# Staged loads in four transfers, g over h in PSUM, and three banks for h: linear attention and a cosine feed-forward layer in one kernel

## The chip, the cores and the metric

The kernel runs on one core of a Trainium2 chip. The metric is the device time of one execution in microseconds (us). The engines are TensorE (PE, matrix products into PSUM), VectorE (DVE), ScalarE (ACT), GpSimd (POOL) and SyncE (SP, which here issues most of the DMA transfers). PSUM has eight banks of 512 fp32 words per partition.

## The reference

The first half is a recurrent linear attention over 768 tokens, with 4 batches of 8 heads of 48 dimensions. The second half is a feed-forward layer on its output, laid out as 3072 tokens by 384.

```
for t in range(S):
    kt, vt, rt = k[:, :, t], v[:, :, t], r[:, :, t]
    cur = einsum('bhd,bhe->bhde', u * kt, vt)
    y[:, :, t] = einsum('bhd,bhde->bhe', rt, state + cur)
    state = w * state + einsum('bhd,bhe->bhde', kt, vt)
x = y as (B*S, H*D)
h = x @ w_in            # 3072 x 384 by 384 x 2048
g = h * cos(h)
out = g @ w_out         # 2048 x 384
```

The weights w_in and w_out come as 64-bit floats; everything else is fp32.

## The kernel before, in words

**Feed-forward.** Each fp32 factor is split into a high and a low part in the type fp32r, and three products replace one. The 24 chunks of 128 tokens form eight blocks of three. A step is one block and one slice f of 128 of the 2048 hidden columns, so there are 128 steps. The first four blocks are walked in four groups of slices (CUTS, L31), so that weights can be converted while the work goes on; the other four take all 16 slices at once. A step is:

- `h` (mm_h, L322): nine matmuls into one PSUM bank, the buffer `ph`
- `qi` on ACT (L342) and `rest` on DVE (L345): h/2pi less its whole part, into `q`, a slot of the SBUF ring `f`
- `cos` on ACT (L348), in place in `q`
- the gate on DVE (f_gate, L1240): g = `ph` times `q`, written over `q` (a block of two chunks would write over `ph`; there is none)
- `gh` on ACT (L1243): g rounded to fp32r; `gl` on DVE (L1246): g less `gh`
- `o` (mm_o, L333): nine matmuls that add the step's share to three accumulator banks

After a block's last slice of a group the accumulators are copied to slots of the ring `f` (L1280 on ACT, L1282 on DVE) and stored by SP, or added to the output by POOL (L1296).

**Attention.** Chunks 0 to 11 (`chunk`, L702) hold 128 tokens of one batch. Chunks 12 to 23 (`late_chunk`, L918) hold 64 tokens of each of two batches. A late chunk needs k and r transposed, with head dimensions on partitions. It loads them in a second, *staged* form (load_s, L940) into slots of the ring `raw`, which has two slots and also serves the weights. DVE transposes them in 32x32 blocks (tr_s, L977, the transpose itself at L980), and POOL multiplies the decay in (decay_s, L984 and L987). The plain loads of k, r and v (load, L931, issued at L934) follow in SP's queue; r goes to a slot of the ring `f`. POOL makes the bonus from them (L999, L1002) and decays k (L1005). PE makes the scores and the state's increment (mm_az, L1035), DVE masks the scores (L1072), and PE makes x (mm_xx, L1095), which ACT and DVE split (L1141, L1146).

**Staged layout.** For each of four 32-row groups n and each batch b, one transfer fills 16 partitions, each with 4 tokens of four heads: 64 pieces of 768 bytes, eight transfers per tensor. In the last chunk the last transfer would run past the tensor's end, so POOL clears a corner (L960) and that transfer is cut into three.

**PSUM.** Banks 0 to 2 are accumulators. h uses banks 3, 4 and 5 in blocks 0 to 3 (B_HX) and banks 3 and 4 in blocks 4 to 7 (B_H). Late attention uses a pair of banks, 5-6 or 6-7 (P_ATT); single banks for small work come from 5 to 7 (B_ATT). The early chunks take any of seven banks (B_EARLY).

**Order.** Every piece of work is an `op` (L90) with an engine, a due time, a cost, a latency, and the buffers it uses. The class `Plan` simulates the engines at build time and hands out buffers by the simulated time at which they are free. `order` (L179) makes 60 tries: after the first ones, `change` (L201) shifts the due times of the best so far at random, for ops due before time 120; each try is replayed with random delays (`replay`, L159), and the best is kept. Its order is written into the instruction streams, so each engine runs its instructions strictly in this order. An op with `port=True` is planned not to overlap another such op, on DVE or POOL. The staged loads are planned with cost 3.9 and latency 3.0, the plain ones with 1.3 and 2.6.

```
P_ATT = [Tile(bank_all[:, i : i + 2], bank[i : i + 2]) for i in (5, 6)]
B_ACC, B_H, B_ATT = bank[0:3], bank[3:5], bank[5:8]
B_HX = bank[3:6]
```

Of the kernel before, what the change touches and what calls it, by code (L numbers as in the profile page):

```python
# [262 lines left out]
def kernel(  # L263
# [17 lines left out]
    P = 128  # L281
# [36 lines left out]
    def f32(ap):  # L318
        return ap.bitcast(F32)
# [31 lines left out]
    with ExitStack() as actx:  # L351
# [4 lines left out]
        bank = [Tile(bank_all[:, i]) for i in range(8)]  # L356
        P_ATT = [Tile(bank_all[:, i : i + 2], bank[i : i + 2]) for i in (5, 6)]
        B_ACC, B_H, B_ATT = bank[0:3], bank[3:5], bank[5:8]
        B_HX = bank[3:6]
        B_EARLY = bank[5:8] + bank[3:5] + bank[0:2]  # L360
# [334 lines left out]

        def staged(buf):
            return f32(buf()).rearrange("q f w -> q (f w)").rearrange("q (p x) -> q p x", p=NP)

# [219 lines left out]
        def late_chunk(i, due, xbuf):  # L918
# [21 lines left out]
            def load_s(buf, src):  # L940
                def part(n, b, q, n_q, p, n_p, n_d):
                    j, d0 = n // 2, 32 * (n % 2)
                    at = 32 * n + 16 * b + q
                    nc.sync.dma_start(  # L944
                        staged(buf)[at : at + n_q, p : p + n_p, 0:n_d],
                        bass.AP(
                            tensor=src.tensor,
                            offset=src.offset + (((2 * m + b) * H + 2 * p + j) * S + t0 + 4 * q) * D + d0,
                            ap=[[4 * D, n_q], [2 * S * D, n_p], [1, n_d]],
                        ),  # L950
                    )

                def go():
                    for n in range(4):
                        for b in range(2):
                            if i < NJ - 1 or n < 3 or b == 0:
                                part(n, b, 0, 16, 0, NP, 4 * D)
                            else:

                                nc.gpsimd.memset(staged(buf)[96:P, NP - 1, 4 * D - 32 :], 0.0)  # L960
                                part(n, b, 0, 16, 0, NP - 1, 4 * D)
                                part(n, b, 0, 15, NP - 1, 1, 4 * D)
                                part(n, b, 15, 1, NP - 1, 1, 4 * D - 32)

                return go
# [4 lines left out]
            ahead = [last_A[0]]  # L970
            l_ks = op(SP, due - 6.2, 3.9, load_s(ks, k), ahead, [ks], lat=3.0, line="late")
            l_rs = op(SP, due - 6.1, 3.9, load_s(rs, r), ahead, [rs], lat=3.0, line="late")
            l_k = op(SP, due - 5.2, 1.3, load(kb, k), ahead, [kb], lat=2.6, line="late")
# [3 lines left out]
            def tr_s(dst, src):  # L977
                def go():
                    blocks = staged(src).rearrange("q p (g x) -> q p g x", g=4)[:, :, :, 0:32]
                    nc.vector.transpose(dst().rearrange("q p (t g) -> q p g t", g=4), blocks)  # L980

                return go

            def decay_s(dst, dec):  # L984
                def go():
                    d = dst()[0:KP].rearrange("q p (b t) -> q p b t", b=2)
                    nc.gpsimd.tensor_tensor(  # L987
                        d, d, dec[0:KP, :, None, mid].to_broadcast([KP, NP, 2, CT]), op=ALU.mult
                    )

                return go
# [43 lines left out]
            def mm_az():  # L1035
                for p in range(NP):
                    for j in range(2):
                        ps = slice(j * DP, j * DP + D)
                        for b in range(2):
                            nc.tensor.matmul(  # L1040
                                score(j)[half[b], p, :],
                                kT()[ps, p, half[b]],
                                rT()[ps, p, half[b]],
                                start=True,
                                stop=True,
                            )
# [48 lines left out]
            def mm_xx():  # L1095
                x = xp()[:, :, 0 : NK * CT].rearrange("q b (kk t) -> q b kk t", kk=NK)
                for kk in range(NK):
                    for b in range(2):
                        for g in range(4 * kk, 4 * kk + 4):
                            p, s = divmod(g, 3)  # L1100
                            gs = slice(G * (g % 4), G * (g % 4) + G)
                            nc.tensor.matmul(  # L1102
                                x[gs, b, kk, :],
                                zb()[:, b, p, G * s : G * s + G],
                                rT()[0:KP, p, half[b]],
                                start=(kk == 0),
                                stop=False,
                                skip_group_check=True,
                            )
# [91 lines left out]
        for s, (n, f, f0, f1) in enumerate(steps):  # L1201
# [21 lines left out]
            for t, cs in enumerate(cols):  # L1223
# [12 lines left out]

                g = ph if nt == 2 else q

# [13 lines left out]
                o6 = op(ACT, dd + 1.2, 0.42 * one, f_gh, [o5], [g, gh], line="gh")  # L1252
                o7 = op(DVE, dd + 1.4, 0.48 * one, f_gl, [o6], [g, gh, gl], line="gl", port=g is q, lat=0.35)
                gs_.setdefault(s, []).append(o7)
# [211 lines left out]
```

## Time and profile before

| | |
|---|---|
| median of 3 runs | 514.33 us (514.09 to 515.32) |
| profiled execution | 515.86 us |
| its span, first to last instruction | 514.1 us |
| PE, DVE, ACT, POOL busy | 500.0, 384.7, 332.3, 175.6 us |
| mean granted TensorE clock | 0.996 |
| bytes moved by DMA | 61.74 MB in 117319 packets |

Busy time counts an instruction from its start to its end, and neighbouring instructions of PE and DVE overlap, so a busy engine may still have short waits inside. In a timeline row the columns are start and duration in us, engine, line and operation, output and inputs, shape and count; a bracket gives the idle time of the engine before it and what ended it. In the table by stretches each engine's busy time stands with its number of instructions, then the granted clock, the DMA share and GB/s. A group row ends in busy us, mean ns of one, and the idle time before them with its releasers.

### The profile page before, as it was taken

Reading aid. Unit: us, or ns where it says so; the run is one execution under the profiler, and the core shown is the slowest. Engines: PE = TensorE matmul, PEld = TensorE weight load, DVE = VectorE, ACT = ScalarE, POOL = GpSimd, SP = SyncE. Lnnn points to the kernel's source line nnn. Section 1 sums busy time; section 2 is a strip of 40 time slices with the busy share of each in tenths; the row PEclk is TensorE's granted clock in tenths of the full one; section 3 lists DMA queues with packets and bytes.
Section 4 is the critical chain, followed back from the end, with each engine's and each line's share of the span. In section 5 each row is a group of like instructions: output and inputs, shape, how many; then the busy total and the mean of one; then the engine's idle time right before and its main releaser. Section 6 shows DMA issues by size and latency. Waiting matters only on the chain.

```text
span 514.1 us, 14178 instructions
## 1 busy us (share of the span) xinstructions
PE 500.0 (97%) x5464; PEld 476.3 (93%) x5464; DVE 384.7 (75%) x777; ACT 332.3 (65%) x834; POOL 175.6 (34%) x186
## 2 busy tenths in 40 slices
PE   8899999999999999999999999999999999999995
PEld 6688899999999999999989999999999899889994
DVE  6789988889988877667786877777766776577552
ACT  3899987776777756547565765666756657375452
POOL 6767522265345443224325134132241322400000
PEclk9999999999999999999999999999999999999998
DMA  8997345478664576325666665374553653520001
GB/s 139 190 186 145 71 140 185 138 157 168 137 134 113 140 143 118 55 59 80 155 114 155 133 161 135 85 193 113 143 136 94 185 121 98 149 58 24 1 1 50
DMA packets 117319, 61.74 MB, mean 120 GB/s; under 512 B 80765, under 2 KB 113150, under 8 KB 117246
## 3 DMA queue, kind: packets, MB, share of 16 engines
q1 hardware_dynamic: 111982, 53.60, 42.8%
q0 software_dynamic: 5184, 7.08, 10.0%
q8 instruction: 44, 0.72, 0.6%
q14 instruction: 29, 0.24, 0.2%
q10 hardware_dynamic: 80, 0.10, 0.1%
HBM read 48.96 MB, written 11.80 MB: 118 GB/s over the span
## 4 chain that ended last, share of the span: by engine, by line
PE 78%; DMA 6%; DVE 4%; ACT 4%; issue 2%; SPq 2%; POOL 1%; DVEq 0%; ACTq 0%; POOLq 0%
PE bank L337 34%; PE bank L331 33%; PE bank L815 2%; DMA raw<-in_r_dram 1%; PE bank L1102 1%; PE bank L1124 1%; SPq L944 1%; ACT A L805 1%; PE bank L741 1%; PE bank L849 1%; DMA f<-in_r_dram 1%; DMA v<-in_v_dram 1%; DVE f L345 1%; PE bank L1040 1%; PE bank L836 1%
## 5 line engine op out<-in xcount | busy, mean ns | idle before, releaser
L337 PE MATMUL bank<-w_out_hi,gh 128*128 128x384 f32 x384 | 132.0, 344 | 0.6 <-DVE f L1282 0.6
L331 PE MATMUL bank<-xh,w_in_hi 128*128 128x384 f32 x384 | 129.8, 338 | 1.9 <-DVE f L1240 1.9
L337 PE MATMUL bank<-w_out_hi,gl 128*128 128x384 f32 x384 | 130.0, 338 | 0.2 <-DVE gl L1246 0.2
L331 PE MATMUL bank<-xh,w_in_lo 128*128 128x384 f32 x384 | 129.5, 337 | 0.0
L337 PE MATMUL bank<-w_out_lo,gh 128*128 128x384 f32 x384 | 129.4, 337 | 0.0
L331 PE MATMUL bank<-xl,w_in_hi 128*128 128x384 f32 x384 | 128.7, 335 | 0.0
L348 ACT ACTIVATE f<-f 128x384 f32<-128x384 f32 (+1 forms) x132 | 67.4, 513 | 49.2 <-DVE f L345 48.6
L1246 DVE TENSOR_TENSOR gl<-f,gh 128x384 fp32r<-128x384 f32 (+1 forms) x132 | 81.8, 621 | 22.6 <-ACT gh L1243 22.1
L345 DVE SCALAR_TENSOR_TENSOR f<-bank,qi 128x384 f32<-128x384 f32 (+1 forms) x132 | 71.0, 540 | 34.0 <-ACT qi L342 29.3
L342 ACT ACTIVATE qi<-bank 128x384 int32<-128x384 f32 (+1 forms) x132 | 62.7, 478 | 47.4 <-PE bank L331 46.6
L1240 DVE TENSOR_TENSOR f<-bank,f 128x384 f32<-128x384 f32 (+1 forms) x132 | 70.9, 540 | 28.4 <-ACT f L348 26.5
L1243 ACT CAST gh<-f 128x384 fp32r<-128x384 f32 (+1 forms) x132 | 65.7, 500 | 40.7 <-DVE f L1240 39.8
L331 PEld LDWEIGHTS bank<-xh,w_in_hi 128*128 128x128 f32 x384 | 72.1, 188 | 3.5 <-DVE f L1240 2.9
L337 PEld LDWEIGHTS bank<-w_out_hi,gh 128*128 128x128 f32 x384 | 72.0, 187 | 3.3 <-DVE f L1282 0.9
L337 PEld LDWEIGHTS bank<-w_out_hi,gl 128*128 128x128 f32 x384 | 72.0, 188 | 0.9 <-DVE gl L1246 0.9
L331 PEld LDWEIGHTS bank<-xh,w_in_lo 128*128 128x128 f32 x384 | 72.1, 188 | 0.0
L331 PEld LDWEIGHTS bank<-xl,w_in_hi 128*128 128x128 f32 x384 | 72.1, 188 | 0.0
L337 PEld LDWEIGHTS bank<-w_out_lo,gh 128*128 128x128 f32 x384 | 72.0, 188 | 0.0
L667 POOL TENSOR_TENSOR f<-f,raw 128x384 int32<-128x384 int32 x32 | 34.8, 1087 | 62.0 <-DVE f L656 43.7
L987 POOL TENSOR_TENSOR kT<-kT,decT_k 112x512 f32<-112x512 f32 x12 | 15.6, 1298 | 103.6 <-DVE kT L980 103.5
L1296 POOL DMA_DIRECT2D out_dram<-f x36 | 33.2, 1019 | 31.8 <-ACT f L1280 23.1
L805 ACT ACTIVATE A<-ident,a 128x128 f32<-128x128 f32 x96 | 30.2, 392 | 3.4 <-DVE a L796 3.4
(112 smaller groups left out, 617.5 us busy)
## 6 DMA issues: line engine op xcount, KB each, us to landing
raw<-in_moe_w_in_dram SPq DMA_DIRECT2D x32, 384.0 KB, 3.8
raw<-in_moe_w_out_dram SPq DMA_DIRECT2D x32, 384.0 KB, 3.8
out_dram<-f POOLq DMA_DIRECT2D x36, 192.0 KB, 4.3
raw<-in_k_dram SPq DMA_DIRECT2D x95, 48.0 KB, 2.6
raw<-in_r_dram SPq DMA_DIRECT2D x95, 48.0 KB, 2.1
k<-in_k_dram SPq DMA_DIRECT2D x12, 192.0 KB, 3.7
r<-in_r_dram SPq DMA_DIRECT2D x12, 192.0 KB, 4.6
v<-in_v_dram SPq DMA_DIRECT2D x12, 192.0 KB, 5.0
```

The lines of the kernel that those rows point to most:

```text
L331: nc.tensor.matmul(ph, a, b_, start=(i == 0), stop=(i == len(mm) - 1))
L337: nc.tensor.matmul(acc, a[:, ts], b_[:, f, :], start=(first and i == 0), stop=(last and i == 2))
L342: nc.scalar.activation(qi, ph, AF.Copy, scale=INV_2PI, bias=0.25)
L345: nc.vector.scalar_tensor_tensor(q, ph, INV_2PI, qi, op0=ALU.mult, op1=ALU.subtract)
L348: nc.scalar.activation(q, q, AF.Sin, scale=TWO_PI, bias=0.5 * math.pi)
L667: lambda: nc.gpsimd.tensor_tensor(ai(), ai(), cn(), op=ALU.add),
L805: nc.scalar.activation(A[j]()[:, p, :], ident, AF.Copy, scale=ab()[:, h : h + 1])
L987: nc.gpsimd.tensor_tensor(d, d, dec[0:KP, :, None, mid].to_broadcast([KP, NP, 2, CT]), op=ALU.mult)
L1240: nc.vector.tensor_tensor(g()[:, cs], ph()[:, cs], q()[:, cs], op=ALU.mult)
L1243: nc.scalar.copy(gh()[:, cs], g()[:, cs])
L1246: nc.vector.tensor_tensor(gl()[:, cs], g()[:, cs], f32(gh())[:, cs], op=ALU.subtract)
L1296: nc.gpsimd.dma_start(to, ob()[rows], accum_op=ALU.add)
```

## The change

There are three edits, in one kernel.

- Staged loads: a partition holds two tokens of eight heads, four of each of the chunk's two batches. The transpose needs 32 words of each token, so a piece reaches from the first of these to the last, D + 32 = 80 words (320 bytes). One transfer per group n fills 32 partitions with 8 such pieces each: four transfers per tensor instead of eight, six instead of ten in the last chunk. The transposed tiles kT and rT are now ordered by batch, pair and token instead of pair, batch and token; the same bytes are read by the decay and the matmuls through other strides. The planned cost is 2.2 instead of 3.9 and the latency 3.5 instead of 3.0.
- The gate writes g over h in PSUM for every step. `gh` and `gl` read it there, so `ph` is held until `gl`, and the slot of `q` is free after the gate. `gl` is no longer planned with `port=True`.
- Banks: h has 3, 4 and 7 for all blocks; late attention has the pair 5-6; B_ATT is 5 and 6.

```diff
-        P_ATT = [Tile(bank_all[:, i : i + 2], bank[i : i + 2]) for i in (5, 6)]
-        B_ACC, B_H, B_ATT = bank[0:3], bank[3:5], bank[5:8]
-        B_HX = bank[3:6]
+        P_ATT = [Tile(bank_all[:, 5:7], bank[5:7])]
+        B_ACC, B_H, B_ATT = bank[0:3], bank[3:5] + bank[7:8], bank[5:7]
+        B_HX = B_H
...
-                def part(n, b, q, n_q, p, n_p, n_d):
-                    j, d0 = n // 2, 32 * (n % 2)
-                    at = 32 * n + 16 * b + q
+                def part(n, e, n_e, q, n_q, n_d):
                     nc.sync.dma_start(
-                        staged(buf)[at : at + n_q, p : p + n_p, 0:n_d],
+                        pieces(buf)[32 * n + q : 32 * n + q + n_q, e : e + n_e, 0:n_d],
...
-                            ap=[[4 * D, n_q], [2 * S * D, n_p], [1, n_d]],
+                            ap=[[2 * D, n_q], [2 * S * D, n_e], [1, n_d]],
...
-                        for b in range(2):
-                            if i < NJ - 1 or n < 3 or b == 0:
-                                part(n, b, 0, 16, 0, NP, 4 * D)
+                        if i < NJ - 1 or n < 3:
+                            part(n, 0, H, 0, 32, D + 32)
+                        else:
+                            nc.gpsimd.memset(pieces(buf)[96:P, H - 1, 2 * D - 32 : D + 32], 0.0)
+                            part(n, 0, H - 1, 0, 32, D + 32)
+                            part(n, H - 1, 1, 0, 31, D + 32)
+                            part(n, H - 1, 1, 31, 1, 2 * D - 32)
...
-            l_ks = op(SP, due - 6.2, 3.9, load_s(ks, k), ahead, [ks], lat=3.0, line="late")
-            l_rs = op(SP, due - 6.1, 3.9, load_s(rs, r), ahead, [rs], lat=3.0, line="late")
+            l_ks = op(SP, due - 6.2, 2.2, load_s(ks, k), ahead, [ks], lat=3.5, line="late")
+            l_rs = op(SP, due - 6.1, 2.2, load_s(rs, r), ahead, [rs], lat=3.5, line="late")
...
-                    blocks = staged(src).rearrange("q p (g x) -> q p g x", g=4)[:, :, :, 0:32]
-                    nc.vector.transpose(dst().rearrange("q p (t g) -> q p g t", g=4), blocks)
+                    blocks = pieces(src).rearrange("q e (g x) -> q e g x", g=2)[:, :, :, 0:32]
+                    to = dst().rearrange("q p c -> q (p c)").rearrange("q (e t g) -> q e g t", e=H, g=2)
+                    nc.vector.transpose(to, blocks)
...
-                g = ph if nt == 2 else q
+                g = ph
...
-                    o7 = op(DVE, dd + 1.4, 0.48 * one, f_gl, [o6], [g, gh, gl], line="gl", port=g is q, lat=0.35)
+                    o7 = op(DVE, dd + 1.4, 0.48 * one, f_gl, [o6], [g, gh, gl], line="gl", lat=0.35)
```

More of the change, by code (lines that the diff above doesn't have):

```diff
@@ L694, in heads, with pieces, late_t @@
             return buf().rearrange("q (h d) -> q h d", h=H)
-        def staged(buf):
-            return f32(buf()).rearrange("q f w -> q (f w)").rearrange("q (p x) -> q p x", p=NP)
+        def pieces(buf):
+            return f32(buf()).rearrange("q f w -> q (f w)").rearrange("q (e x) -> q e x", e=H)
+        def late_t(buf):
+            return buf().rearrange("q p c -> q (p c)").rearrange("q (b p t) -> q b p t", b=2, p=NP)
         def cube(buf):
@@ L940, in load_s @@
             def load_s(buf, src):
-                def part(n, b, q, n_q, p, n_p, n_d):
-                    j, d0 = n // 2, 32 * (n % 2)
-                    at = 32 * n + 16 * b + q
+                def part(n, e, n_e, q, n_q, n_d):
                     nc.sync.dma_start(
-                        staged(buf)[at : at + n_q, p : p + n_p, 0:n_d],
+                        pieces(buf)[32 * n + q : 32 * n + q + n_q, e : e + n_e, 0:n_d],
                         bass.AP(
                             tensor=src.tensor,
-                            offset=src.offset + (((2 * m + b) * H + 2 * p + j) * S + t0 + 4 * q) * D + d0,
-                            ap=[[4 * D, n_q], [2 * S * D, n_p], [1, n_d]],
+                            offset=src.offset + ((2 * m * H + 2 * e + n // 2) * S + t0 + 2 * q) * D + 32 * (n % 2),
+                            ap=[[2 * D, n_q], [2 * S * D, n_e], [1, n_d]],
                         ),
@@ L954, in go @@
                     for n in range(4):
-                        for b in range(2):
-                            if i < NJ - 1 or n < 3 or b == 0:
-                                part(n, b, 0, 16, 0, NP, 4 * D)
[L958 to L963, printed above, removed]
+                        if i < NJ - 1 or n < 3:
[5 more added lines that the diff above has]
+                            part(n, H - 1, 1, 31, 1, 2 * D - 32)
                 return go
@@ L985, in go @@
                 def go():
-                    d = dst()[0:KP].rearrange("q p (b t) -> q p b t", b=2)
+                    d = late_t(dst)[0:KP]
                     nc.gpsimd.tensor_tensor(
-                        d, d, dec[0:KP, :, None, mid].to_broadcast([KP, NP, 2, CT]), op=ALU.mult
+                        d, d, dec[0:KP, None, :, mid].to_broadcast([KP, 2, NP, CT]), op=ALU.mult
                     )
@@ L1041, in mm_az @@
                                 score(j)[half[b], p, :],
-                                kT()[ps, p, half[b]],
-                                rT()[ps, p, half[b]],
+                                late_t(kT)[ps, b, p, :],
+                                late_t(rT)[ps, b, p, :],
                                 start=True,
@@ L1104, in mm_xx @@
                                 zb()[:, b, p, G * s : G * s + G],
-                                rT()[0:KP, p, half[b]],
+                                late_t(rT)[0:KP, b, p, :],
                                 start=(kk == 0),
```

## The prediction

> **What bounds the kernel now.** I read the page's shares first, then the busy time by stretches, then the timeline of TensorE (PE), and last the timelines of the engines that PE waited for.
>
> ```profile
> span 514.1 us, 14178 instructions
> ...
> PE 500.0 (97%) x5464; PEld 476.3 (93%) x5464; DVE 384.7 (75%) x777; ACT 332.3 (65%) x834; POOL 175.6 (34%) x186
> ```
> ```profile
> core 0: us, PE busy (x) PEld busy (x) DVE busy (x) ACT busy (x) POOL busy (x), PEclk, DMA share, GB/s
> 0.00:36.00 36.00, 31.79 (x493) 25.36 (x494) 27.20 (x61) 24.50 (x71) 25.60 (x42) 1.00 1.07 174
> 36.00:78.00 42.00, 41.94 (x703) 36.68 (x702) 38.74 (x78) 38.13 (x104) 22.25 (x21) 1.00 0.51 117
> 78.00:215.00 137.00, 137.00 (x786) 136.78 (x785) 115.11 (x223) 94.22 (x212) 55.80 (x57) 1.00 0.60 136
> 215.00:460.00 245.00, 241.57 (x3216) 230.23 (x3215) 175.11 (x354) 150.54 (x390) 71.95 (x67) 1.00 0.53 126
> 460.00:508.00 48.00, 47.72 (x274) 47.30 (x272) 28.52 (x66) 24.67 (x60) 0.00 (x0) 1.00 0.04 10
> 508.00:514.00 6.00, 0.00 (x0) 0.00 (x0) 0.00 (x0) 0.23 (x1) 0.00 (x0) 0.71 0.41 104
> ```
>
> PE is busy 97% of the span and the change takes no matmul away, so only the other 14 us can move. The stretches say where they are: 4.21 us before 36 us (loads and the first attention chunks), 0.06 to 78 us, nothing to 215 us, 3.43 us between 215 and 460 us, where the twelve late chunks run, 0.28 us to 508 us, and 6 us of draining, in which the last copy and store run. The change works on the fourth row. There PE has four visible pauses and some that hide between rows:
>
> ```profile
> 259.67 0.45 PE L337 MATMUL bank<-w_out_hi,gh 128*128 128x384 f32 x1 [0.61 <-DVE f L1282]
> ...
> 302.07 0.69 PE L1040 MATMUL bank<-rT,kT 48*64 48x64 f32 x32 [0.41 <-POOL rT L987]
> ...
> 404.81 0.44 PE L331 MATMUL bank<-xh,w_in_hi 128*128 128x384 f32 x1 [0.68 <-DVE f L1240]
> ...
> 442.89 0.45 PE L331 MATMUL bank<-xh,w_in_hi 128*128 128x384 f32 x1 [1.25 <-DVE f L1240]
> ...
> 449.57 0.34 PE L337 MATMUL bank<-w_out_hi,gh 128*128 128x384 f32 x1
> 449.96 0.44 PE L337 MATMUL bank<-w_out_hi,gl 128*128 128x384 f32 x1
> ```
>
> The bracket is PE's idle time and its releaser: 0.61 + 0.41 + 0.68 + 1.25 = 2.95 of the 3.43 us. A matmul after a pause takes 0.44 instead of 0.34, so each pause costs 0.1 more. Rows also overlap: 449.57 to 449.96 is 0.39 us between starts where 128x384 matmuls otherwise start 0.17 apart (worked out under the banks), a pause of 0.2 with no bracket. By the start times there are some 0.7 us of these between 449 and 456 us. Together 2.95 + 0.4 + 0.7, about 4.0 us.
>
> Each has its cause on DVE or POOL, whose instructions run in the order written:
>
> ```profile
> 256.25 2.90 DVE L1246 TENSOR_TENSOR gl<-f,gh 128x384 fp32r<-128x384 f32 x1
> ...
> 403.05 0.56 DVE L345 SCALAR_TENSOR_TENSOR f<-bank,qi 128x384 f32<-128x384 f32 x1 [2.04 <-POOL f L999]
> ...
> 441.37 1.08 DVE L980 STREAM_TRANSPOSE rT<-raw 128x512 f32<-128x512 f32 x1 [3.28 <-DMA raw<-in_r_dram]
> ```
> ```profile
> 256.46 1.30 POOL L1005 TENSOR_TENSOR k<-k,dec_k 128x384 f32<-128x384 f32 x1
> ...
> 299.44 1.02 POOL L999 TENSOR_TENSOR f<-f,k 128x384 f32<-128x384 f32 x1 [5.01 <-DMA f<-in_r_dram]
> 300.41 1.60 POOL L987 TENSOR_TENSOR rT<-rT,decT_r 112x512 f32<-112x512 f32 x1
> ...
> 402.00 1.01 POOL L999 TENSOR_TENSOR f<-f,k 128x384 f32<-128x384 f32 x1 [4.58 <-DMA f<-in_r_dram]
> ...
> 438.74 0.12 POOL L960 MEMSET raw<- 32x32 f32 x1 [5.39 <-ACT f L348]
> ```
>
> The pause at 259 us: a `gl` of 2.90 us beside POOL's L1005, and the copy L1282 that frees PE's accumulator stood behind it. At 301 and 404 us: POOL waited 5.01 and 4.58 us for the plain load of r, which SP issues behind the staged loads; L987 and, through a slot of the ring `f`, DVE's L345 stood behind. At 442 us: DVE stood 3.28 us before the transpose of the staged r, the gate L1240 behind it, and h waits for the bank that the gate frees; the pauses at 449 us are the backlog.
>
> **The staged loads.** Per tensor, eight transfers of 48 KB become four of 80 KB: 16 partitions by 4 pieces of 768 bytes become 32 by 8 of 320.
>
> ```profile
> 409.91 3.62 SPq L944 DMA_DIRECT2D raw<-in_k_dram  x8
> 413.63 4.55 SPq L944 DMA_DIRECT2D raw<-in_r_dram  x8
> ...
> 433.01 6.51 SPq L944 DMA_DIRECT2D raw<-in_r_dram  x10
> ```
> ```profile
> L944 SPq DMA_DIRECT2D raw<-in_r_dram x98: 252/424/1542, 182.7 to 439.3; - x98
> ```
> ```profile
> L934 SPq DMA_DIRECT2D f<-in_r_dram x24: 595/610/701, 188.0 to 441.7; - x24
> ```
> ```profile
> raw<-in_k_dram SPq DMA_DIRECT2D x95, 48.0 KB, 2.6
> raw<-in_r_dram SPq DMA_DIRECT2D x95, 48.0 KB, 2.1
> ...
> f<-in_r_dram SPq DMA_DIRECT2D x24, 96.0 KB, 3.2
> ```
>
> An issue costs SP 0.42 us (64 pieces) or 0.61 us (L934, 512 pieces of 192 bytes); one of 256 pieces lies between, and I take 0.55. Four take 2.2 us (1.7 to 2.4) where eight took 3.62 and 4.55, so the two staged loads leave SP 8.2 - 4.4 = 3.8 us sooner, and the three plain loads behind them too. The landing is 2.1 to 2.6 us for the old form and 3.2 for L934's small pieces; I take 2.9, keeping 2.1 and 3.2 for the range. From the first issue to the data: 2.2 + 2.9 = 5.1 us instead of about 4.1 + 2.4 = 6.5. The planner, which writes the order of every engine, is told 2.2 + 3.5 = 5.7 instead of 3.9 + 3.0 = 6.9: what comes on time before comes with 0.6 us to spare after. The last chunk is the exception. Its loads are cut round a POOL memset, which for r came at 438.74, 5.7 us after the first issue, and held the last three back: ten issues in 6.51 us; six will take about 6.51 - 4 x 0.42 = 4.8, still more than the planner's 2.2. The two pauses from the plain loads of r should go, 0.41 + 0.68 + 0.2 = 1.3 us. The third, in the last chunk, may leave a part.
>
> [...]
>
> **g in PSUM.** The gate writes over h; `gh` and `gl` read it there; `gl` then has one SBUF input instead of two.
>
> ```profile
> L1246 DVE TENSOR_TENSOR gl<-f,gh 128x384 fp32r<-128x384 f32 (+1 forms) x132 | 81.8, 621 | 22.6 <-ACT gh L1243 22.1
> ...
> L1243 ACT CAST gh<-f 128x384 fp32r<-128x384 f32 (+1 forms) x132 | 65.7, 500 | 40.7 <-DVE f L1240 39.8
> ...
> L1280 ACT COPY f<-bank 128x384 f32<-128x384 f32 x40 | 19.0, 475 | 8.8 <-PE bank L337 7.5 <-DVE f L578 0.5 <-issue 0.4
> ```
> ```profile
> L1240 DVE TENSOR_TENSOR f<-bank,f 128x384 f32<-128x384 f32 x13 | 7.2, 555 | 5.0 <-ACT f L348 4.7
> ...
> L1246 DVE TENSOR_TENSOR gl<-f,gh 128x384 fp32r<-128x384 f32 x12 | 6.7, 556 | 6.0 <-ACT gh L1243 6.0
> ```
>
> The second fence is 462 to 498 us, when POOL does nothing: `gl` from SBUF 556 ns, the gate from PSUM 555. Over the whole run `gl` averages 621 and can reach 2.90 us beside POOL. So I price `gl` at 555 ns: 132 x 66 ns = 8.7 us less of DVE time, all beside PE's work, and the pause at 259 us goes, 0.61 + 0.1 = 0.7 us. `gh` from PSUM takes about 475 instead of 500, by L1280. No row shows DVE writing PSUM; the reads cost nothing extra, so I take zero and bound it by 25 ns either way, the difference that ACT shows. That would be 3 us over 132 gates, beside PE's work. The transposes write at half the former stride; I keep 1.08 us for them.
>
> [...]
>
> **Three banks for h.** Blocks 4 to 7 had two banks for h, freed by the gate; now all have three, freed by `gl`. By the rows below three steps take 128.73 - 119.31 = 9.42 us, so a step 3.14 and each of its 18 matmuls 0.174. With two banks the gate had to end 6.3 us after its h began, and `gl` now has 9.4 us: one period more, for two operations more. The attention loses nothing: the pairs 5-6 and 6-7 shared bank 6, so one pair at a time was in use already. Blocks 0 to 3 had three banks freed by the gate and are now tighter; in the present order the smallest margin between 80 and 215 us is this one:
>
> ```profile
> 119.31 0.33 PE L331 MATMUL bank<-xh,w_in_hi 128*128 128x384 f32 x1
> ...
> 128.73 0.33 PE L331 MATMUL bank<-xh,w_in_hi 128*128 128x384 f32 x1
> ```
> ```profile
> 126.46 1.20 DVE L1246 TENSOR_TENSOR gl<-f,gh 128x384 fp32r<-128x384 f32 x1
> ```
>
> The `gl` of the step at 119.31 ends at 127.66, and the h that will need its bank starts at 128.73: 1.07 us to spare. So I cost the longer hold at nothing. If that cover goes, h waits for the excess. For the last chunk the third bank takes most of 1.25 us away, but o, which needs `gl` too, is late next: I count 1.0 of 1.35 there and 0.35 of the 0.7 behind it.
>
> **Sum.** 0.7 + 1.3 + 1.0 + 0.35 = 3.35 us. The order is planned anew, and I expect one pause such as that at 404 us somewhere else: 0.68 back, which leaves 2.7 us. The profiled execution took 515.86 us around a span of 514.1; it would become 513.2, its span 511.4. The median of the runs is 514.33, 1.5 less than the profiled one; taking the same off gives **511.6 us**. About 0.3%, 1.5 us, is what a measurement of this kernel can tell from no change.
>
> **Rivals.** *A, the new order eats it.* The search that makes the order (`change`, L201) shifts at random what is due before 120 us, so the first 36 us, with 4.21 us of idle PE, come out otherwise. Where half the late gain, 1.4, stays and the start idles 1.0 us more, the time is 513.9. For it: the start has no slack. Against: its loads and costs are unchanged. *B, the small pieces land late.* The wait of 3.28 us on the transpose cost h 1.25, so some 2.0 are hidden. The planner expects data 5.7 us after the first issue; with 2.2 of issue, a landing beyond 5.5 us (5.7 + 2.0 - 2.2) makes PE wait. At 5.9 each of the 24 transposes costs 0.4, 9.6 us; less the 2.3 us of load pauses that are there now (0.41 + 0.68 + 1.25) and the 0.7 of `gl`, the time is 520.9. Against it stands the 3.2 of L934. [...] *C, h waits for `gl`.* It decides from 9.4 us after h's start. The same DVE wait would have to fall where `gl` is already as late as in the quoted step (8.35 us): 8.35 + 3.28 is 2.2 over; three such cost 6.6, and with the gain 518.2.
>
> **How the numbers follow.** The forecast has 0.70, A 0.21, B 0.05, C 0.04. The range runs from all 4.0 us gone and the start 1.5 us better (508.8) to A with 0.4 of the late gain left (514.9). Faster by over 0.3% is the forecast, 0.70; within 0.3% is A, 0.21; slower is B and C, 0.09.
>
> **What would show it.** Right: the PE row for 215 to 460 us rises to the stretch's length within about 1 us; `gl` averages 540 to 560 ns with no outlier near 2.9; L944's issues halve, at 0.42 to 0.61; no transpose waits over 1 us except in the last chunk. Wrong: landings of the staged loads above 3.5 us; h waiting for L1246; more than 5.2 us of PE idle before 36 us, which is A; a gate well over 555 ns.

## The result and the profile after

The changed kernel takes 510.81 us (median of 4 runs, 510.69 to 511.69); the kernel before, run beside it, takes 514.3 (514.09 to 515.32). The ratio is 0.9932, with an interval of 0.9915 to 0.9949: a gain of 3.5 us, more than a measurement of this kernel can miss. The profiled execution took 510.79 us, its span is 509.0 where it was 514.1.

The head of the page and the busy time by stretches of the changed kernel, the last stretch set so that it ends with PE's work (columns as before):

```profile
span 509.0 us, 14020 instructions
...
PE 498.1 (98%) x5464; PEld 476.6 (94%) x5464; DVE 370.3 (73%) x777; ACT 326.8 (64%) x834; POOL 173.8 (34%) x186
```
```profile
0.00:36.00 36.00, 31.93 (x472) 25.44 (x474) 26.98 (x62) 24.21 (x70) 25.91 (x43) 1.00 1.08 172
36.00:78.00 42.00, 41.67 (x723) 36.34 (x722) 38.12 (x78) 37.48 (x103) 22.89 (x22) 1.00 0.51 121
78.00:215.00 137.00, 137.00 (x788) 137.00 (x787) 111.01 (x221) 92.76 (x213) 55.05 (x57) 1.00 0.60 134
215.00:460.00 245.00, 245.00 (x3248) 236.05 (x3247) 169.74 (x365) 151.49 (x399) 69.90 (x67) 1.00 0.53 122
460.00:503.00 43.00, 42.46 (x243) 41.76 (x241) 24.45 (x56) 20.87 (x52) 0.00 (x0) 1.00 0.01 3
```

The fourth row is the result: between 215 and 460 us PE is now busy for all of the 245.00 us, where it missed 3.43. The other rows stand nearly as they did; before 36 us PE idles 4.07 us instead of 4.21.

Busy time hides what lies between two rows that overlap, so the runs below are compared by a second measure. It cuts the span at two matmuls: the first matmul of step 48, which is the 49th group of nine at L331, and the last matmul of PE (its start and 0.17 us). What lies ahead of the first is called the front, from there to the second the late part; the drain behind it is 6.5 to 7.3 us in every run. The two rows of PE's timeline in the kernel before, and in the changed one:

```profile
210.37 0.33 PE L331 MATMUL bank<-xh,w_in_hi 128*128 128x384 f32 x1
...
507.38 0.34 PE L337 MATMUL bank<-w_out_lo,gh 128*128 128x384 f32 x1
```
```profile
210.60 0.33 PE L331 MATMUL bank<-xh,w_in_hi 128*128 128x384 f32 x1
...
502.12 0.34 PE L337 MATMUL bank<-w_out_lo,gh 128*128 128x384 f32 x1
```

The late part took 507.55 - 210.37 = 297.18 us and now takes 502.29 - 210.60 = 291.69: 5.49 us less, while the front is 0.23 longer. So between these two executions all of the gain is in the late part. By the medians it is 3.5 us: the profiled execution of the kernel before lies 1.5 above its median, and where in that execution the 1.5 us were lost isn't known.

The work that the edits touch: first the gate in the kernel before, then, in the changed kernel, groups of the page, the answers for the lines of the staged loads and of the transposes (count, shortest/median/longest duration in ns, first and last start), and the page's rows of the staged loads (KB each, median us to landing).

```profile
L1240 DVE TENSOR_TENSOR f<-bank,f 128x384 f32<-128x384 f32 (+1 forms) x132 | 70.9, 540 | 28.4 <-ACT f L348 26.5
```
```profile
L1241 DVE TENSOR_TENSOR bank<-bank,f 128x384 f32<-128x384 f32 (+1 forms) x132 | 72.6, 550 | 37.4 <-ACT f L348 34.5
...
L1247 DVE TENSOR_TENSOR gl<-bank,gh 128x384 fp32r<-128x384 f32 (+1 forms) x132 | 71.0, 539 | 26.4 <-ACT gh L1244 26.1
L1244 ACT CAST gh<-bank 128x384 fp32r<-128x384 f32 (+1 forms) x132 | 61.7, 467 | 39.1 <-DVE bank L1241 37.1
```
```profile
L945 SPq DMA_DIRECT2D raw<-in_r_dram x50: 241/451/1682, 176.2 to 427.3; - x50
...
DMA to landing us min/median/max: 1.9/2.5/4.6
```
```profile
L981 DVE STREAM_TRANSPOSE rT<-raw x12: 702/704/715, 182.5 to 429.4; 128x512 f32<-128x512 f32 x12
```
```profile
raw<-in_k_dram SPq DMA_DIRECT2D x47, 80.0 KB, 2.4
raw<-in_r_dram SPq DMA_DIRECT2D x47, 80.0 KB, 3.1
```

The gate into PSUM takes 550 ns where it took 540 into SBUF, `gl` 539 instead of 621, `gh` 467 instead of 500. A transfer of the staged r costs SP 0.45 us to issue. Over k and r a transfer lands in 2.5 us, where the old form landed in 1.5/2.4/4.7; k's alone lands a little sooner (2.4 instead of 2.6) and r's later (3.1 instead of 2.1). What became shorter is the issuing, in SP's timeline of the changed kernel, here for the last chunk but one and for the last:

```profile
401.27 1.86 SPq L945 DMA_DIRECT2D raw<-in_k_dram  x4
...
406.08 1.80 SPq L945 DMA_DIRECT2D raw<-in_r_dram  x4
...
421.71 2.50 SPq L945 DMA_DIRECT2D raw<-in_k_dram  x6
...
424.31 3.35 SPq L945 DMA_DIRECT2D raw<-in_r_dram  x6
```

1.86 + 1.80 = 3.66 us for two tensors, where two took 3.62 + 4.55 = 8.17; and 3.35 us for r in the last chunk, where it was 6.51. The two rows that stood behind these loads, POOL's wait for the plain r (from the views of waits: idle us, times, longest; the kernel before, then the changed one), and the last transpose:

```profile
POOL f L999 <- DMA f<-in_r_dram: 17.5, 8, 5.0
```
```profile
POOL f L1000 <- DMA f<-in_r_dram: 7.5, 7, 2.7
```
```profile
429.41 0.71 DVE L981 STREAM_TRANSPOSE rT<-raw 128x512 f32<-128x512 f32 x1 [0.43 <-DMA raw<-in_r_dram]
```

The last transpose waited 0.43 us where it waited 3.28.

### The profile page after: what moved, and what is told of

The parts are those of the page before. It is cut to its first block, busy times and chain, and to the rows that moved or that the text cites. A ratio compares the mean times of both kernels' runs of the same rounds, so it can differ in the third digit from the quotient of the medians.

```text
span 509.0 us, 14020 instructions
## 1 busy us (share of the span) xinstructions
PE 498.1 (98%) x5464; PEld 476.6 (94%) x5464; DVE 370.3 (73%) x777; ACT 326.8 (64%) x834; POOL 173.8 (34%) x186
## 4 chain that ended last, share of the span: by engine, by line
PE 91%; ACT 3%; DVE 1%; DMA 1%; POOL 1%; SPq 1%; issue 0%; POOLq 0%; ACTq 0%; DVEq 0%
PE bank L337 41%; PE bank L331 39%; ACT A L808 2%; PE bank L1103 2%; PE bank L1125 2%; PE bank L818 2%; PE bank L1041 1%; PE bank L852 1%; DMA k<-in_k_dram 1%; PE bank L744 1%; PE bank L839 1%; PE bank L1054 1%; DVE A L825 0%; PE bank L874 0%; DVE a L799 0%
## 5 line engine op out<-in xcount | busy, mean ns | idle before, releaser
L331 PE MATMUL bank<-xh,w_in_lo 128*128 128x384 f32 x384 | 129.6, 338 | 0.0
L331 PE MATMUL bank<-xh,w_in_hi 128*128 128x384 f32 x384 | 129.1, 336 | 0.3 <-ACT A L808 0.2
L331 PE MATMUL bank<-xl,w_in_hi 128*128 128x384 f32 x384 | 128.7, 335 | 0.0
L1241 DVE TENSOR_TENSOR bank<-bank,f 128x384 f32<-128x384 f32 (+1 forms) x132 | 72.6, 550 | 37.4 <-ACT f L348 34.5
L1247 DVE TENSOR_TENSOR gl<-bank,gh 128x384 fp32r<-128x384 f32 (+1 forms) x132 | 71.0, 539 | 26.4 <-ACT gh L1244 26.1
L1244 ACT CAST gh<-bank 128x384 fp32r<-128x384 f32 (+1 forms) x132 | 61.7, 467 | 39.1 <-DVE bank L1241 37.1
L331 PEld LDWEIGHTS bank<-xh,w_in_hi 128*128 128x128 f32 x384 | 72.1, 188 | 0.9 <-ACT A L808 0.3
L331 PEld LDWEIGHTS bank<-xh,w_in_lo 128*128 128x128 f32 x384 | 72.2, 188 | 0.0
L331 PEld LDWEIGHTS bank<-xl,w_in_hi 128*128 128x128 f32 x384 | 72.1, 188 | 0.0
```

Of the source, the lines that this page charges most:

```text
L331: nc.tensor.matmul(ph, a, b_, start=(i == 0), stop=(i == len(mm) - 1))
L1241: nc.vector.tensor_tensor(g()[:, cs], ph()[:, cs], q()[:, cs], op=ALU.mult)
L1244: nc.scalar.copy(gh()[:, cs], g()[:, cs])
L1247: nc.vector.tensor_tensor(gl()[:, cs], g()[:, cs], f32(gh())[:, cs], op=ALU.subtract)
```

## The experiments

Three explanations fit this. By the first, the prediction's, each edit removes its own pauses: the loads some, `gl` from PSUM another, the third bank most of the one in the last chunk. By the second, the loads alone do it. By the third nothing does: the changed costs make the search find another order, and this one happens to be good. The runs were made on three other chips, where the kernel before had medians of 516.52 (e1, e2, e3, e6), 517.47 (e4, e5, e8, e10) and 516.85 us (e7, e9, e11, e12). So the parts of the trace are compared, each from one profiled execution, and totals only by their ratios, which are as recorded and not the quotients of two medians:

| kernel | median us | ratio to before | front us | late us | PE busy, 215 to 460 |
|---|---|---|---|---|---|
| before | 514.33 | | 210.37 | 297.18 | 241.57 |
| after | 510.81 | 0.9932 (0.9915 to 0.9949) | 210.60 | 291.69 | 245.00 |
| e1 before again | 517.69 | 1.0017 (0.9994 to 1.0039) | 210.75 | 297.81 | 241.28 |
| e2 loads alone | 513.86 | 0.9951 (0.9930 to 0.9972) | 213.85 | 291.84 | 244.74 |
| e3 g in PSUM and banks | 513.54 | 0.9946 (0.9921 to 0.9971) | 208.44 | 295.05 | 242.36 |
| e4 g in PSUM alone | 520.20 | 1.0055 (1.0027 to 1.0083) | 210.05 | 301.43 | 238.89 |
| e5 banks alone | 515.15 | 0.9964 (0.9939 to 0.9990) | 209.63 | 296.17 | 242.00 |
| e6 before, planned slower | 523.08 | 1.0124 (1.0085 to 1.0163) | 210.57 | 304.60 | 237.82 |
| e7 before, quick transposes | 516.81 | 1.0004 (0.9978 to 1.0030) | 212.40 | 298.50 | 241.30 |
| e8 after, other seed | 511.08 | 0.9895 (0.9839 to 0.9951) | 210.31 | 291.71 | 245.00 |
| e9 after, old planned costs | 509.88 | 0.9877 (0.9839 to 0.9916) | 209.60 | 291.65 | 245.00 |
| e10 before, other seed | 514.47 | 0.9959 (0.9928 to 0.9989) | 209.25 | 297.08 | 241.38 |
| e11 after, more tries | 510.66 | 0.9893 (0.9859 to 0.9926) | 209.98 | 291.68 | 245.00 |
| e12 after, slow transposes | 511.15 | 0.9902 (0.9869 to 0.9936) | 210.40 | 291.69 | 245.00 |

The kernel before is 2 to 3 us slower on these chips than on the first; the four runs with all three edits (e8, e9, e11, e12) are not. Here they lie 5.7 to 7.0 us below its medians, where the first chip showed 3.5. So the size of the gain hangs on the chip or the occasion, and why isn't shown.

**e1: the kernel before, unchanged,** as a measure of what repeats.

> The kernel before, unchanged, profiled and timed once more. It measures what varies from one execution to the next: the profiled execution shown took 515.86 us, 1.5 more than the median. If the pauses between 215 and 460 us are set by the written order, they come again at the same instructions and PE idles about 3.4 us there. If they hang on when single loads land, some shrink or vanish, 1.5 to 3.0 us idle, and the profiled time is nearer 514.3. The ratio should be 1.000 within 0.002.

```profile
215.00:460.00 245.00, 241.28 (x3212) 229.75 (x3211) 174.54 (x354) 150.25 (x389) 72.62 (x67) 1.00 0.54 125
```

The same row of the stretches: PE misses 3.72 us here and 3.43 in the first trace, and the late part differs by 0.63 us. The kernels e7 and e10 below, which from step 48 on run the same order as the kernel before, have 298.50 and 297.08. So a difference of up to some 1.4 us in the late part can be chance, and the median is 0.17% from that of the other runs of the same kernel, so 0.2% in a total can be too.

**e2: the loads alone.** The changed kernel with the old banks and with g in SBUF again (and `gl` planned with `port=True` again).

```diff
-        P_ATT = [Tile(bank_all[:, 5:7], bank[5:7])]
-        B_ACC, B_H, B_ATT = bank[0:3], bank[3:5] + bank[7:8], bank[5:7]
-        B_HX = B_H
+        P_ATT = [Tile(bank_all[:, i : i + 2], bank[i : i + 2]) for i in (5, 6)]
+        B_ACC, B_H, B_ATT = bank[0:3], bank[3:5], bank[5:8]
+        B_HX = bank[3:6]
...
-                g = ph
+                g = ph if nt == 2 else q
...
```

> Only the staged loads in four transfers (layout, transposes and planned costs with them); g stays in SBUF, banks as before. Theory (late loads and a slowed gl, each with its own pauses): the three load pauses of 0.41, 0.68 and 1.25 us and the backlog of 0.7 go, gl still has stretched cases above 2 us beside POOL and keeps 0.5 to 1.3 us idle between 215 and 460 us; time about 512.2. Rival 'third bank': without it h still waits for the gate, idle stays at 2.5 us or more, about 514. Rival 'lottery of the order': anything from 512 to 516, with the idle time at new places.

```profile
215.00:460.00 245.00, 244.74 (x3244) 235.09 (x3243) 176.51 (x363) 154.64 (x398) 76.25 (x69) 1.00 0.53 120
```
```profile
L1247 DVE TENSOR_TENSOR gl<-f,gh 128x384 fp32r<-128x384 f32 (+1 forms) x132 | 82.2, 626 | 23.7 <-ACT gh L1244 22.7
```
```profile
DVE rT L981 <- DMA raw<-in_r_dram: 4.7, 4, 1.9
```

The late part is 291.84 us: 5.34 of the 5.49 us are there with the old banks and with a `gl` that takes 626 ns, near the 621 of the kernel before. I had expected such a `gl` to keep 0.5 to 1.3 us of PE idle; it misses 0.26. DVE still waits for the staged r (third fence, from the view of waits), but 1.9 us at most. The total hides the gain, since the front of this order is 3.25 us longer than that of the changed kernel (its reason is in the last section).

**e3: the other two edits alone,** put into the kernel before (`gl` planned without `port`, as in the changed kernel).

```diff
-        P_ATT = [Tile(bank_all[:, i : i + 2], bank[i : i + 2]) for i in (5, 6)]
-        B_ACC, B_H, B_ATT = bank[0:3], bank[3:5], bank[5:8]
-        B_HX = bank[3:6]
+        P_ATT = [Tile(bank_all[:, 5:7], bank[5:7])]
+        B_ACC, B_H, B_ATT = bank[0:3], bank[3:5] + bank[7:8], bank[5:7]
+        B_HX = B_H
...
-                g = ph if nt == 2 else q
+                g = ph
...
```

> Only g over h in PSUM and three banks for h; the staged loads stay at eight transfers. Theory: gl at 550 ns, the 0.61 pause gone, L980 still waits 3 us for r in the last chunk and POOL's L999 some 5 us for its r, but the third bank hides part: 1.0 to 2.0 us idle between 215 and 460 us, time about 512.8. Rival 'third bank': it hides all of it, idle under 0.5 us, time 511. Rival 'lottery': no relation to the edits, 512 to 516.

```profile
440.90 0.69 PE L1040 MATMUL bank<-rT,kT 48*64 48x64 f32 x32 [2.20 <-POOL rT L987]
```

PE misses 2.64 us, where 1.0 to 2.0 were expected. The total is as good as that of e2, but for another reason: the front is 2.3 us shorter than in e1, the late part 2.13 us shorter than before. The row of PE's timeline says what is left: the third bank lets h go on in the last chunk, and then the scores wait 2.20 us for the transposed r, which still comes late. The wait is moved from h to the scores and not removed.

**e4: g in PSUM alone,** with the old banks (`gl` planned without `port`).

```diff
-                g = ph if nt == 2 else q
+                g = ph
...
```

> Only g over h in PSUM (and gl planned without the shared port); banks and staged loads as before. Blocks 4 to 7 then have two banks for h, held until gl instead of until the gate. Theory: gl needs 1.2 to 1.6 us more than the gate, and the quoted steps of before had 0.05 to 2.2 us to spare between a gate and the h that takes its bank, so h waits in most late steps: 0.3 to 1 us in 30 to 60 of 64 steps, from the step 48 to PE's end 310 to 340 us instead of 297, time 525 to 560. Rival 'gl alone': the shorter gl gains what it gains and the hold costs nothing, 296 us and about 513.

From the view of waits, and one row of PE's timeline:

```profile
PE bank L331 <- DVE gl L1246: 6.6, 8, 1.6
```
```profile
437.80 0.44 PE L331 MATMUL bank<-xh,w_in_hi 128*128 128x384 f32 x1 [1.59 <-DVE gl L1246]
```

Two banks held until `gl` make h wait for `gl`, eight times and 6.6 us in all; the late part grows by 4.25 us. I had expected much more, a time of 525 to 560 us, because I priced the longer hold into the old order. The order is planned anew round the hold; that it costs only where the plan finds nothing to put in its place is my reading and not tested.

**e5: the banks alone,** with g in SBUF.

```diff
-        P_ATT = [Tile(bank_all[:, i : i + 2], bank[i : i + 2]) for i in (5, 6)]
-        B_ACC, B_H, B_ATT = bank[0:3], bank[3:5], bank[5:8]
-        B_HX = bank[3:6]
+        P_ATT = [Tile(bank_all[:, 5:7], bank[5:7])]
+        B_ACC, B_H, B_ATT = bank[0:3], bank[3:5] + bank[7:8], bank[5:7]
+        B_HX = B_H
```

> Only the third bank for h; g stays in SBUF and gl may be stretched beside POOL; staged loads as before. Theory: the waits of h for the gate (2.1 us with their restarts) go, the 0.61 of gl stays, POOL's and o's waits stay: from step 48 to PE's end about 294.5 us instead of 297.2. Rival 'gl is what counts': no gain here, 297. The front up to step 48 may differ by some 2 us either way, as in the runs so far (208.4, 210.6, 213.9), and is not put down to the edit.

The late part is 1.01 us shorter than before, which can be chance; 2.7 were expected. PE's largest wait of the last chunk is again one for the transposed r:

```profile
PE bank L1040 <- POOL rT L987: 1.1, 1, 1.1
```

Together the runs form a square. In the late part g in PSUM costs 4.25 us with the old banks, and with the new ones it doesn't cost (296.17 and 295.05, a difference that can be chance). The third bank is what g in PSUM needs; neither adds to what the loads give, since e2 and the changed kernel are 0.15 us apart.

**e6: the kernel before, with its planner told more of the truth.** The two staged loads of a chunk took 8.17 us to issue in the quoted rows, and the plan counts on 2 x 3.9; here it counts on 2 x 4.4. If the kernel before suffers because its plan expects the data too early, this should mend it.

```diff
-            l_ks = op(SP, due - 6.2, 3.9, load_s(ks, k), ahead, [ks], lat=3.0, line="late")
-            l_rs = op(SP, due - 6.1, 3.9, load_s(rs, r), ahead, [rs], lat=3.0, line="late")
+            l_ks = op(SP, due - 6.2, 4.4, load_s(ks, k), ahead, [ks], lat=3.0, line="late")
+            l_rs = op(SP, due - 6.1, 4.4, load_s(rs, r), ahead, [rs], lat=3.0, line="late")
```

> The kernel before with one number changed: the planner is told 4.4 instead of 3.9 us for a staged load, what SP needs in the trace (3.6 to 4.7). Nothing that runs is changed but the order. If the load pauses come from a plan that expects the data too early, the idle time between 215 and 460 us falls to 1.0 to 2.0 us and the time to about 513. If the eight transfers are simply too long to fit, it stays at 3 us and 514.3. By the 'lottery' it changes by up to 1.5 us either way, most of it before 80 us.

It made it 1.24% slower, with a late part of 304.60 us. DVE still waits for a staged load, for as long as before, and PE behind it. Here the transpose is that of k; the profile names r's load as the releaser, but r's issues begin only at 399.26, as those of k end:

```profile
400.83 1.08 DVE L980 STREAM_TRANSPOSE kT<-raw 128x512 f32<-128x512 f32 x1 [3.27 <-DMA raw<-in_r_dram]
```
```profile
403.51 0.45 PE L331 MATMUL bank<-xh,w_in_hi 128*128 128x384 f32 x1 [2.67 <-DVE f L1240]
```

So telling the plan this cost does not mend it; e9 below is the test from the other side. No expectation covered this: PE misses 7.2 us, and why this order is the worst of all is open.

**e7: the kernel before, with quicker transposes.** The transposes took 1.10 us before and take 0.70 after, which I hadn't expected. Here the kernel before writes them densely. This puts tokens of the late chunks in another order, so the late attention computes something else; the amount of work is the same.

```diff
-                    nc.vector.transpose(dst().rearrange("q p (t g) -> q p g t", g=4), blocks)
+                    nc.vector.transpose(dst().rearrange("q p (g t) -> q p g t", g=4), blocks)
```

> The kernel before, with the transposes of the staged k and r writing their 32 words next to each other instead of 16 bytes apart; tokens come out in another order, so the late half of the attention is not the reference's. The transposes took 1.10 us at a stride of 16 bytes and 0.70 at 8. If the stride sets the time, they take 0.70 us or less here (0.5 to 0.7). Theory (it is the arrival of the loads that counts): the waits of L980 for its DMA stay, step 48 to PE's end 296 to 297.5 us. Rival 'the shorter transpose made the gain': 293.5 or less.

```profile
L980 DVE STREAM_TRANSPOSE rT<-raw 128x512 f32<-128x512 f32 x12 | 8.5, 705 | 6.7 <-DMA raw<-in_r_dram 6.7
```

The transposes take 705 ns, and the late part is 298.50 us, no shorter than before: the group still stands 6.7 us waiting for the data (5.0 in the kernel before).

**e8 and e10: the changed kernel and the kernel before with another seed** for the search that makes the order.

```diff
-        rng = random.Random(9)
+        rng = random.Random(10)
```

> The changed kernel with another seed for the order's random tries, nothing else. If the late gain belongs to the edits, step 48 to PE's end stays at 291.7 within 0.7 us, and only the front moves (210.6 within 3 us), time 509 to 514. If the gain was a lucky order, the late part goes back to 294 us or more.

> The kernel before with the same other seed. The late part stays at 297 us within 1.5, with the same kinds of pauses (loads of the last chunk, POOL behind r) at other places; the front moves within 3 us of 210.4. If the late part falls to 293 or less, the old pauses were an accident of one order.

```profile
215.00:460.00 245.00, 245.00 (x3248) 236.05 (x3248) 170.90 (x365) 151.96 (x399) 69.67 (x67) 1.00 0.54 122
```
```profile
215.00:460.00 245.00, 241.38 (x3216) 230.54 (x3216) 178.15 (x356) 151.24 (x391) 72.08 (x66) 1.00 0.54 125
```

With another seed the changed kernel again fills the stretch (first row, e8) and the kernel before misses 3.62 us (second row, e10); the late parts are 291.71 and 297.08. But this is no test of the third explanation in the late part. The seed shifts only what is due before 120 us, and from step 48 on the trace of e10 has the same lines in the same order as the kernel before on PE, DVE, ACT and POOL; e8 differs from the changed kernel in a few neighbours swapped on DVE and ACT. Each run repeats one late order. What speaks against luck there are runs whose late order is their own, e2 above and e9 below. The front is another matter: the two fronts of the kernel before are 1.12 us apart, part of the 2.1 us (0.41%) by which e10's ratio stands below 1.

**e9 and e11: the changed kernel with the old planned costs, and with four times as many tries.**

```diff
-            l_ks = op(SP, due - 6.2, 2.2, load_s(ks, k), ahead, [ks], lat=3.5, line="late")
-            l_rs = op(SP, due - 6.1, 2.2, load_s(rs, r), ahead, [rs], lat=3.5, line="late")
+            l_ks = op(SP, due - 6.2, 3.9, load_s(ks, k), ahead, [ks], lat=3.0, line="late")
+            l_rs = op(SP, due - 6.1, 3.9, load_s(rs, r), ahead, [rs], lat=3.0, line="late")
```
```diff
-PASSES = 60
+PASSES = 240
```

> The changed kernel, its planner told the old 3.9 and 3.0 us for a staged load that now takes SP 1.8. The data come sooner than planned. If the true arrival makes the gain, step 48 to PE's end stays within 0.7 us of 291.7. If the plan's numbers make it (the order they lead to), it goes back towards 297, as the kernel told 4.4 went to 304.6.

> The changed kernel with 240 instead of 60 tries for the order, as a version that may beat both. The late part has no pause left, so it stays at 291.7; only the front can gain, from 210.6 down to some 208.5, the best seen so far (208.4). Time 508.5 to 511. By the rival 'the planner's picture of the front is not good enough', more tries change it at random, 209 to 213.

The late parts are 291.65 and 291.68 us: the changed numbers of the plan do nothing there. e9's late order differs from the changed kernel's on every engine, so it also speaks against a lucky order; e11's is nearly the changed kernel's again. Both fronts are somewhat shorter than that of the changed kernel (209.60 and 209.98 against 210.60); the 208.5 that I hoped for in e11 did not come. e9 has the lowest median, 509.88 us, but the interval of its ratio, 0.9839 to 0.9916, holds the ratios of e8 and e11 too, so it isn't shown to be better than the changed kernel.

**e12: the changed kernel with transposes that write 16 bytes apart,** as the kernel before does. Here too the tokens of the late chunks come in another order.

```diff
-                    blocks = pieces(src).rearrange("q e (g x) -> q e g x", g=2)[:, :, :, 0:32]
-                    to = dst().rearrange("q p c -> q (p c)").rearrange("q (e t g) -> q e g t", e=H, g=2)
+                    flat_s = f32(src()).rearrange("q f w -> q (f w)")
+                    blocks = flat_s.rearrange("q (a c x) -> q a c x", a=4, c=4)[:, :, :, 0:32]
+                    to = dst().rearrange("q p c -> q (p c)").rearrange("q (a t c) -> q a c t", a=4, c=4)
```

> The changed kernel with the transposes writing 16 bytes apart again, as before the change (four transfers, g in PSUM and three banks stay); tokens come out in another order, so the late half of the attention is not the reference's. If the stride sets the time, the transposes take 1.10 us again. Theory: step 48 to PE's end stays at 291.7 to 292.5 us, since 24 x 0.4 us of DVE time lie beside PE's work. Rival 'the shorter transpose made the gain': 294 or more.

```profile
L982 DVE STREAM_TRANSPOSE rT<-raw x12: 1086/1094/1109, 182.3 to 429.2; 128x512 f32<-128x512 f32 x12
```

The transposes are slow again, and the late part stays at 291.69. With e7 this takes the shorter transposes out of the reasons.

What is left, by these runs, is the earlier staged data: fewer issues in SP's queue ahead of it. All kernels with the four transfers have a late part of 291.65 to 291.84 us, in three different late orders (the changed kernel's, e2's, e9's), and none with eight is below 295.05, in five (the kernel before's, e3 to e6). The transposes' waits for staged data divide the kernels in the same way: in each kernel with eight transfers DVE stands 2.8 to 3.8 us in front of some transpose, in those with four 1.9 us at most. The plain loads do not divide them: POOL's waits for the plain r come to 7.5 us in the changed kernel and 12.8 in e2, to 17.5 in the kernel before but 2.4 in e6.

That the gain comes by way of the issuing is read from the views (8.17 to 3.66 us, the landing no sooner) and not tested by itself. The four transfers also carry fewer bytes, 320 KB a tensor instead of 384, and smaller pieces. Four transfers with the old pieces of 768 bytes, eight with an earlier place in SP's queue, and eight shared with another queue were not tried.

## Why the prediction was right, point by point

**The bound and the place** were right. PE was the bound, the pauses of the fourth stretch could go, and they are all that went.

**The load pauses** (1.3 us) went, and SP is free 4.5 us sooner in the quoted chunk where 3.8 were forecast. The price of an issue was taken at 0.55 and is 0.45; of landing at 2.9 and is 2.5 (3.1 for r alone). The bounds from the two nearest rows held both. The last chunk's r was put at 4.8 us of issuing and took 3.35. Of the mechanism, the staged data is what the runs bear out; that the plain r's coming sooner removed a pause is not shown, since e2 removes both pauses with POOL's waits for it at 12.8 us in all.

**The size is the term that was off.** The pauses to be had were put at 4.0 us, from brackets and from rows around 449 us; the late part fell by 5.49. A busy row that starts late after its neighbour shows no bracket, and I worked out such lost starts for one stretch of 7 us only. Of the 4.0 us that I found I took 3.35, and the whole went: in the last chunk not 1.0 of 1.35 and 0.35 of 0.7 but all.

**The attribution to `gl` and to the third bank** failed. The 0.7 us of the pause at 259 us were put down to `gl` from PSUM; e2 has the old `gl`, 626 ns, and PE misses 0.26 us in the whole stretch. The 1.0 us in the last chunk was put down to the third bank; e3 has that bank, and PE waits 2.20 us for r there. The rows show both causes in the order of the kernel before. That another order puts other work beside a long `gl` is my reading; that late data stays late is shown for five orders, by the transposes' waits of 2.8 us and more.

**"One pause somewhere else: 0.68 back"** did not come. PE has no pause between 215 and 460 us.

**The profiled execution and the median.** I carried the 1.5 us by which the kernel before's profiled execution lay over its median to the changed kernel. The changed kernel's lies on its median, 510.79 and 510.81. So the profiled execution fell by 5.1 us, where 2.7 was forecast, and the median by 3.5. That the forecast of 511.6 is only 0.8 from the median is in part luck: two terms, the gain and that offset, erred in opposite ways.

**The longer hold at nothing** was right with three banks: no matmul of h waits for `gl` in the changed kernel. e4 shows the price of the cover, 6.6 us of such waits with two. **The price of DVE writing PSUM** was taken as zero, between 25 ns either way; it is 10 ns, 550 for a gate where it was 540. (The 555 in the prediction is of full-size gates alone; the 132 of the page hold six smaller ones in both kernels.) **The transposes** were kept at 1.08 us and take 0.70, a miss without effect (e12).

**The rivals.** A, the new order: e2 is such a case, with its front 3.25 us longer and the late gain whole; that the late gain would be halved was wrong. B, the small pieces land late: the landing is 2.5 us, for r 3.1, against the 5.5 from which it would decide. Over k and r, transfers of 80 KB in 320-byte pieces land in 2.5 us, within 0.1 of the 2.4 of those of 48 KB in 768-byte ones. The 3.1 us of r alone, 1.0 more than before, leave room for a small effect. C, h waits for `gl`: it is the mechanism of e4, and the third bank keeps it away.

## What to carry to other kernels

Where an order is planned anew with every edit, follow a pause back to what comes again in every order, here data that leaves its queue late (2.8 us and more in front of a transpose, in five orders), and price that first; a pause whose releaser is a slow instruction beside other work may vanish with any edit, as the 0.61 us behind `gl` did (e2 misses 0.26 in the whole stretch, with `gl` still at 626 ns). Count a DMA queue by its issues: here eight transfers of 48 KB held up everything behind them more (3.62 and 4.55 us of issuing) than four of 80 KB with pieces less than half as long did (1.86 and 1.80). Cut the span at an instruction that both kernels have, as step 48 here: the late part repeats to 0.1 us in the five kernels with all three edits, while the fronts of all the runs lie between 208.44 and 213.85 for reasons of their own. And before a new seed is taken for a new order, compare the orders: here it left the late part's order as it was.

## What the runs showed of the hardware

**The transposes that write 16 bytes apart took longer, 1.10 us against 0.70.** The DVE transpose of 128x512 fp32 took 1.10 us where neighbours are written 16 bytes apart, in the kernel before (first row, for the transposed r) and in e12 (above), and 0.70 both 8 bytes apart (the changed kernel) and dense (second row, e7).

```profile
L980 DVE STREAM_TRANSPOSE rT<-raw x12: 1077/1096/1117, 189.2 to 441.4; 128x512 f32<-128x512 f32 x12
```
```profile
L980 DVE STREAM_TRANSPOSE rT<-raw x12: 700/702/712, 191.3 to 444.8; 128x512 f32<-128x512 f32 x12
```

**Behind some pauses of PE the granted clock was lower, 0.58 and 0.59.** In e6 the pause of 2.67 us at 403.51 is followed by a lower granted clock. In the two stretches around it the clock is the third number from the right:

```profile
400.00:404.00 4.00, 1.33 (x8) 1.01 (x7) 2.49 (x4) 1.41 (x4) 1.26 (x1) 1.00 0.44 107
404.00:408.00 4.00, 4.00 (x16) 4.00 (x15) 3.38 (x6) 2.00 (x5) 1.45 (x1) 0.59 0.57 123
```

PE is busy in all of the second stretch. Of its 16 matmuls two began before it, so it starts 14 where 4 us hold 23 at 0.174: 9 x 0.174 = 1.6 us are lost, and as much by the mean clock of 0.59 (4 x 0.41). Two shorter pauses close together were followed by one too. e7's front runs the same instructions as that of the kernel before, with the first of two pauses 0.36 us longer (first fence the kernel before, then e7, then e7's stretch):

```profile
25.30 0.62 PE L741 MATMUL bank<-ident,r 128*112 128x128 f32 x4 [0.52 <-DMA r<-in_r_dram]
...
27.72 1.16 PE L815 MATMUL bank<-rT,kT 48*128 48x128 f32 x16 [0.72 <-ACT kT L786]
28.81 1.10 PE L849 MATMUL bank<-A,v 128*32 128x128 f32 x32
```
```profile
26.09 0.62 PE L741 MATMUL bank<-ident,r 128*112 128x128 f32 x4 [0.88 <-DMA r<-in_r_dram]
...
28.51 1.97 PE L815 MATMUL bank<-rT,kT 48*128 48x128 f32 x16 [0.72 <-ACT kT L786]
30.41 1.88 PE L849 MATMUL bank<-A,v 128*32 128x128 f32 x32
```
```profile
28.00:32.00 4.00, 3.49 (x48) 3.08 (x48) 2.22 (x6) 2.90 (x9) 3.26 (x4) 0.58 1.04 182
```

The sixteen matmuls of L815 take 1.97 us instead of 1.16, and L849's behind them 1.88 instead of 1.10, at a clock of 0.58. e2's longer front has such a stretch too, behind a pause of 1.76 us; with PE idle for 5.59 us before 36 us instead of 4.07, it makes up most of the 3.25:

```profile
21.87 0.65 PE L744 MATMUL bank<-ident,k 128*112 128x128 f32 x4 [1.76 <-POOL k L771]
```
```profile
24.00:32.00 8.00, 8.00 (x146) 6.68 (x144) 5.80 (x13) 7.78 (x25) 5.85 (x6) 0.82 0.63 147
```

So the lower clock came behind a gap of 2.67 us (0.59 in e6), and behind 0.88 and 0.72 us one after the other (0.58 in e7), but not behind the 0.52 and 0.72 of the kernel before (1.00 from 28 to 32 us). In these runs the length of one gap doesn't decide: behind the 2.20 us of e3 above, longer than e2's 1.76, the matmuls from 441.80 on start 0.17 us apart, as they do elsewhere. What does is open. In e7's front 0.36 us more of waiting was followed by 1.6 us more in the matmuls behind it.
